# Weighted values ahead of the second softmax, norms by pairs of tiles, and four batches of head sums

## The chip, the cores and the metric

The kernel runs on one core of one Trainium2 chip. The metric is the device time of an execution in microseconds (us), as the median of several executions. Beside it there is one profiled execution, from which all durations below are taken.

The engines have the names of the profile: PE is TensorE's matmul, PEld its weight load, DVE is VectorE, ACT is ScalarE, POOL is GpSimd and SP is SyncE, which here only issues DMAs.

## The reference

The input x has 2048 rows of 640 values in bfloat16. It is normalized once, and two blocks work on the result: attention over a dilated window, and a bilinear gate. All is added to x.

```python
xn = layernorm(x)                         # 2048 x 640, no gain or offset
q, k, v = split(xn @ wqkv)                # 32 heads of 20
# each position sees 8 positions: itself and those 2, 4, ... 14 before it
logits = einsum("bhsd,bhswd->bhsw", q, kg) * 20 ** -0.5     # outside: -1e9
o = einsum("bhsw,bhswd->bhsd", softmax(logits), vg)
y = ((xn @ w_gate) * (xn @ w_up)) @ w_down                  # 640 -> 1536 -> 640
out = x + o @ wo + y
```

## The kernel before, in words

The 2048 rows are worked on as 16 tiles of 128 rows (t) for the norm and the output, and as 4 blocks of 512 rows (j) for everything between.

*Order.* No engine's order is written by hand. Every piece of work is a Task with an engine, what it reads and writes, a priority (a small number goes first) and perhaps PSUM banks; the generators (`front`, `proj_qk`, `products`, `softmax`, `weighted`, `gu`, `dn` and others) yield Tasks and conditions. When the program is built, a planner (`Sched`) keeps an estimated time for each engine, takes the Task that can start first in its estimate, by priority among those that can start about equally soon, and appends its instructions to the engine's program. Each instruction has an estimated duration (`occ`), and a DMA an estimated issue time and landing:

```python
self.t[eng] = start + (0.48 if occ is None else occ)
...
self.t_data = max(self.t_data, start + 1.2) + nbytes / 280e3
X.end = self.t_data + 0.8 + extra
```

On the chip each engine runs its program strictly in that order and waits on semaphores for what an instruction needs. Estimates decide the order and nothing else. A Task with `lock=True` is kept from overlapping, in the estimate, with another such Task on VectorE or GpSimd.

*Norm* (`front`). For each tile: two BN statistics and an aggregation on VectorE (L542, L545), a square root on ScalarE (L548), a reciprocal on VectorE (L553), from tile 6 on also minus mean times reciprocal (L556), then the normalization to XNS on VectorE (tiles 0 to 5) or ScalarE (L569). Tiles 0 to 3 are transposed by TensorE (L599), tiles 4 to 15 by transposing DMAs on SP (L632). The result is XNT.

*Projections* (L655, L687). TensorE makes QT and KT for tiles 0 to 3 singly or by pairs, for tiles 4-5 and 6-7 by pairs, and for tiles 8-11 and 12-15 by fours, and values VST by blocks. Values go through a scratch in HBM, since they are wanted shifted and with another layout (VX).

*Logits.* VectorE multiplies queries with shifted keys (L819; for j = 3 in float32 from PSUM, L864). For j = 3 GpSimd adds some of the products (L890, L908) or issues accumulating DMAs (L886). TensorE then sums over a head's values with a 32-column matrix G (L930); four such matmuls run side by side in a 128*32 form. ScalarE copies to LOG (L941).

*Softmax* (`softmax`). Two of them, for j = 0, 1 and for j = 2, 3, on VectorE and ScalarE. Then 16 small DMAs on SP move the weights into ATX, with another layout; `("atx", x)` is marked.

*Weighted values* (`weighted`, `unit`). There are 20 units u = 5 j + c. At c = 0 ScalarE copies the weights of j from ATX into two PSUM banks (L1076) that this step holds from there on. VectorE multiplies VX with them into a slot PV in float32 (L1091), GpSimd adds pairs into a slot SV in bfloat16 (L1096), and TensorE sums over four partition groups with a 32-column matrix SEL (L1144) in batches of units; ScalarE copies to OT (L1153). `BATCH = (1, 4, 9, 14, 19)` names the unit that closes a batch. SV has five slots at first; PV has two until the second softmax is done, then three.

*Gate* (`gu`). For each j, 12 pairs of chains of five matmuls (WG and WU, L1195), each chain into one PSUM bank. ScalarE copies the first into HT, HX or XNT (L660, one helper line for most copies), and VectorE multiplies the second bank onto it (L1204), or ScalarE copies the second bank to UX and GpSimd multiplies (L1221).

*Down products* (`dn`, L1277). For each output tile 12 matmuls with WD and 5 with WO into one bank, a sum with x on VectorE (L1290), and a store.

*Conditions around the change.* `calm` lets GpSimd's locked work start only while no softmax is between its logits and its end. `on_pool` sends a gate product to GpSimd after the second softmax. `vx_loads` begins when the logits of all four blocks are planned.

Of the kernel before, what the change touches and what calls it, by code (L numbers as in the profile page):

```python
# [11 lines left out]
NCH = 5  # L12
# [336 lines left out]
def build_kernel(nc, A_x, A_wqkv, A_wo, B_x, B_w_gate, B_w_up, B_w_down, out):  # L349
# [42 lines left out]
    SV += [sb(f"SV{5 + i}", [128, 4, JB], at=a_ra + i * 4096) for i in range(3)]  # L392
    sv_free = list(range(NS))
    a_sc = place[0]
# [53 lines left out]
    def mark(*k):  # L448
        done.add(k)
# [7 lines left out]
    def num(n, *k):  # L457
        return lambda: count.get(k, 0) >= n
# [4 lines left out]
    def dma(o, i, r=(), w=(), name="", eng="sp", group=None, land=None):  # L463
        n = mybir.dt.size(o.dtype)
        for s in o.shape:
# [7 lines left out]
                                         fill=1.0, base=0, channel_multiplier=1),  # L473
       r=[IDENT[:]], w=[IDENT[:]], name="ident", occ=0.4)
    op("pool", lambda e: e.memset(G[:], 0.0), w=[G[:]], name="g0", occ=0.2)
    op("pool", lambda e: e.affine_select(G[:], G[:], pattern=[[-4, H]], compare_op=ALU.is_gt,
# [57 lines left out]
    def front(t):  # L534
# [9 lines left out]
        def aggr():  # L544
            op("dve", lambda e: e.bn_aggr(mv, st), r=[("st", t, 0), ("st", t, 1)], w=[("mv", t)], name=f"bnag{t}", occ=0.2)  # L545

        def sqrt():
            op("act", lambda e: e.activation(sd, mv[:, 1:2], ACT.Sqrt, bias=EPSC[:, 0:1]), r=[("mv", t), EPSC[:]],  # L548
               w=[("sd", t)], name=f"sd{t}", occ=0.25)
            mark("sd", t)  # L550

        def recip():
            op("dve", lambda e: e.reciprocal(rstd, sd), r=[("sd", t)], w=[("rstd", t)], name=f"rstd{t}", occ=0.16)  # L553
            mark("rstd", t)
            if t >= N_DVE_A:
                op("dve", lambda e: e.tensor_scalar(nmr, mv[:, 0:1], rstd, -1.0, op0=ALU.mult, op1=ALU.mult),  # L556
                   r=[("mv", t), ("rstd", t)], w=[("nmr", t)], name=f"nmr{t}", occ=0.13)

# [25 lines left out]
        yield Task("dve", aggr, r=[("st", t, 1)], prio=p)  # L584
        yield Task("act", sqrt, r=[("mv", t)], prio=p - 1)
        yield Task("dve", recip, r=[("sd", t)], prio=p)
        if t >= NXN:
# [190 lines left out]

    def calm():
        return all(("sm", x) in done or count.get(("logits", x), 0) < 2 for x in range(2))  # L780

# [9 lines left out]
    def products():  # L791
        rows = {j: [] for j in range(NJ)}
        holds = {}
        for j, kind in ORDER:
            if kind == "w":
                if j not in holds:
                    yield from fetch(j, 0, holds.setdefault(j, {c: [] for c in range(4)}))
                yield from wide(j, rows[j], holds[j])
            else:
                if len(QUAD.get(j, ())) == 2 and j not in holds:  # L800
                    yield from fetch(j, 0, holds.setdefault(j, {c: [] for c in range(4)}))
                for r in (1, 0):
                    for c in range(NCH - 1 if r in QUAD.get(j, ()) else 0, NCH):
                        yield from narrow(j, r, c, rows[j])
            if len(rows[j]) == 10 - 3 * len(QUAD.get(j, ())):
                K.spawn(logits(j, rows[j]))

    def narrow(j, r, c, slots):
# [16 lines left out]
    def q_bank(j, c, hold):  # L825
        def go(b):
            mms([(PS[:, b, :], 0, c, j * JB, JB)], b, f"p0_{j * JB}")
            hold.append(b)
            if len(QUAD[j]) == 2:
                for _ in range(4):  # L830
                    bump("qk", 0, j, c)

        def copy():
            evac([(QT[:, j, c, :], PS[:, hold[0], :], JB)], f"qev{j}_{c}")
# [13 lines left out]
    def wide(j, slots, hold):  # L848
        halves = [(r, q0) for r in QUAD[j] for q0 in (0, 2)]
        acc, parts = {}, {1: [], 0: []}  # L850
        for c0 in (0, 2):
            for i, (r, q0) in enumerate(halves):
                f = []
                for c in (c0, c0 + 1):
                    yield lambda: len(hold[c]) > 0 and len(usable(j)) > 0
                    k = slot(j)
                    f.append(k)
                    o = PRD32[k]
                    kv, rk = k_view(j, r, c, q0, 2)
                    q = PS[:, hold[c][0], :]  # L860
                    qb = q.unsqueeze(1).to_broadcast([128, 2, JB])

                    def go(o=o, qb=qb, kv=kv, q=q, rk=rk):
                        X = op("dve", lambda e: e.tensor_tensor(o[:], qb, kv, ALU.mult), r=[q, rk], w=[o[:]],  # L864
                               name=f"prow{j}_{r}_{c}_{q0}", occ=1.17)
# [91 lines left out]
    def softmax(x):  # L957
        def tt(o, a, b, f, name, occ):
            return Task("dve", lambda: op("dve", lambda e: e.tensor_tensor(o, a, b, f), r=[a, b], w=[o], name=name, occ=occ,
                                          lock=True), r=[a, b], w=[o], prio=10, lock=True)  # L960

# [7 lines left out]
        def sub():  # L969
            op("dve", lambda e: e.tensor_tensor(L[:], L[:], bc(M3[:], 8), ALU.subtract), r=[L[:], m3], w=[L[:]], name="lsub",  # L970
               occ=1.2, lock=True)

        def exp():
            op("act", lambda e: e.activation(L[:], L[:], ACT.Exp), r=[L[:]], w=[L[:]], name="exp", occ=1.9)

        def recip():
            op("act", lambda e: e.activation(s3, s3, ACT.Ln), r=[s3], w=[s3], name="rln", occ=0.4)
            op("act", lambda e: e.activation(R, s3, ACT.Exp, scale=-1.0), r=[s3], w=[R], name="rs", occ=0.4)

        def attn():  # L980
            op("dve", lambda e: e.tensor_tensor(L[:], L[:], bc(RS[:], 8), ALU.mult), r=[L[:], R], w=[L[:], ("tok", x)], name="attn",  # L981
               occ=1.2, lock=True)

        def move():
# [6 lines left out]

        yield num(2, "logits", x)
        if x:
            yield have("sm", x - 1)
# [15 lines left out]
    NU = NJ * NCH  # L1010
    BATCH = (1, 4, 9, 14, 19)

    def vx_loads():
        yield num(NJ, "lg")
        for u in range(NU):
# [23 lines left out]
    def weighted():  # L1039
        yield have("atx", 0)  # L1040

        def take(a, b):
            at_bank.extend((a, b))

        yield Task("act", take, banks=2, prio=0, contig=True)
        for u in range(NU):
            yield from unit(u)

    def unit(u):
# [4 lines left out]
        if not more and count.get(("dn", 0), 0) >= 8:  # L1054
            more.append(1)
            sv_free.extend(range(NS, len(SV)))
        yield lambda: len(sv_free) > 0
        sv_of[u] = sv_free.pop(0)
# [13 lines left out]
        v = VX[:, u % NVX]  # L1072

        def at_copy(r):
            o, i = PS[:, at_bank[r], :], ATX[j // 2][:, j % 2, r, :]
            op("act", lambda e: e.activation(o, i, ACT.Copy), r=[i], w=[o], name=f"atp{j}_{r}", occ=0.55)  # L1076

# [31 lines left out]

        if c in (0, NCH - 1):  # L1110
            for r in range(2):
                if c == 0:
                    yield Task("act", lambda: at_copy(r), r=[ATX[j // 2][:, j % 2, r, :]],
                               w=[PS[:, at_bank[r], :]], prio=1)
# [48 lines left out]
    def on_pool(j, m):  # L1163
        return ("sm", 1) in done and m < 11 and ucount[0] - count.get(("hp",), 0) < HP_MAX

    def gu(j):
# [14 lines left out]
        for m in range(NF):  # L1181
# [17 lines left out]
            def after(h=h, hold=hold, j=j, m=m):  # L1199
# [11 lines left out]
                if on_pool(j, m):  # L1211
# [26 lines left out]
    def xr_loads():  # L1238
        yield have("xnt", NT - 1)
        yield have("vx", NVX)  # L1240
# [21 lines left out]
    def dn_piece(j, t, nb, rows, c0, c1):  # L1262
# [48 lines left out]
        K.spawn(tail())  # L1311

    N_PE_T = 4
    BN_AFTER = (4,)
    N_DVE_A = 6
    N_DVE_C = 5
# [23 lines left out]
    def misc():  # L1340
        yield have("xnt", NT - 1)

        def sel():
            for q in range(4):
                a, b = SEL[32 * q:32 * q + 32, :], IDENT[32 * q:32 * q + 32, 32 * q:32 * q + 32]
                op("dve", (lambda a, b: lambda e: e.tensor_copy(a, b))(a, b), r=[b], w=[a], name=f"sel{q}", occ=0.1)
# [5 lines left out]
        yield Task("dve", sel, prio=19)  # L1352
        yield Task("act", lambda: op("act", preload, name="exp_preload", occ=1.3), prio=6)
# [56 lines left out]
```

## Time and profile before

| what | value |
|---|---|
| median of 3 runs | 268.62 us (268.61 to 268.77) |
| the profiled execution, its own time | 268.34 us |
| its span, first to last instruction | 266.8 us |
| clock granted to TensorE | 1.000 |
| TensorE busy | 261.3 us (98%) |
| TensorE weight loads | 152.6 us (57%) |
| VectorE busy | 218.3 us (82%) |
| GpSimd busy | 132.4 us (50%) |
| ScalarE busy | 107.6 us (40%) |

The page gives busy times first, then the span in 40 slices of 6.67 us with a digit for the busy tenths of each, then the DMA queues, then the chain of work that ended last, followed back from the last instruction. In the rows of instruction groups the text before the bar names line, engine, operation, the tile written and those read, shapes and count; after the bar stand the busy time in us, the mean duration of one in ns, and the idle time of the engine just before them, with what ended it. A few per cent of matmul records are missing from a trace: a chain of five then shows four.

### The profile page before, as it was taken

Reading aid. Unit: us, or ns where it says so; the run is one execution under the profiler, and the core shown is the slowest. Engines: PE = TensorE matmul, PEld = TensorE weight load, DVE = VectorE, ACT = ScalarE, POOL = GpSimd, SP = SyncE. Lnnn points to the kernel's source line nnn. Section 1 sums busy time; section 2 is a strip of 40 time slices with the busy share of each in tenths; the row PEclk is TensorE's granted clock in tenths of the full one; section 3 lists DMA queues with packets and bytes.
Section 4 is the critical chain, followed back from the end, with each engine's and each line's share of the span. In section 5 each row is a group of like instructions: output and inputs, shape, how many; then the busy total and the mean of one; then the engine's idle time right before and its main releaser. Section 6 shows DMA issues by size and latency. Waiting matters only on the chain.

```text
span 266.8 us, 4468 instructions
## 1 busy us (share of the span) xinstructions
PE 261.3 (98%) x1771; PEld 152.6 (57%) x1788; DVE 218.3 (82%) x278; ACT 107.6 (40%) x193; POOL 132.4 (50%) x83
## 2 busy tenths in 40 slices
PE   7999999999999999999999999999999999999996
PEld 5996965444444444444444446764577547754775
DVE  4678899999999996379999899988998999981221
ACT  3469998556732122255434442007500460016000
POOL 1000000000007359700399999977999799979000
PEclk9999999999999999999999999999999999999999
DMA  7974789502226997193426733656345633130101
GB/s 213 374 207 81 195 107 371 213 0 98 101 49 161 192 234 178 9 333 81 114 49 142 170 80 87 185 162 168 80 129 152 184 96 89 49 98 2 49 27 49
DMA packets 40933, 35.75 MB, mean 134 GB/s; under 512 B 16080, under 2 KB 39120, under 8 KB 40912
## 3 DMA queue, kind: packets, MB, share of 16 engines
q1 hardware_dynamic: 40096, 33.31, 46.0%
q0 software_dynamic: 576, 2.10, 4.1%
q8 instruction: 14, 0.23, 0.4%
q10 hardware_dynamic: 240, 0.05, 0.1%
q14 instruction: 7, 0.06, 0.1%
HBM read 25.07 MB, written 5.26 MB: 114 GB/s over the span
## 4 chain that ended last, share of the span: by engine, by line
PE 96%; DVE 1%; DMA 1%; issue 1%; ACT 0%
PE PS L1195 39%; PE PS L1277 28%; PE PS L655 22%; PE PS L930 3%; PE PS L687 2%; PE PS L1144 2%; DMA XST<-in_A_x_dram 1%; PE PS L599 0%; DVE STATS L542 0%; ACT XNT L611 0%; DVE XNS L563 0%; DVE XNT L609 0%; DVE FOUT L1290 0%; ACT SD L548 0%; DVE MV L545 0%
## 5 line engine op out<-in xcount | busy, mean ns | idle before, releaser
L1096 POOL TENSOR_TENSOR SV<-PV 128x1024 bf16<-128x1024 f32 x40 | 93.2, 2361 | 20.4 <-DVE LOG L981 19.4
L1091 DVE TENSOR_TENSOR PV<-VX,PS 128x1024 f32<-128x1024 bf16 (+1 forms) x56 | 91.9, 1669 | 2.5 <-POOL SV L1096 2.3
L655 PE MATMUL PS<-XNT,WQKV 128*128 128x512 bf16 (+2 forms) x384 | 60.2, 315 | 0.4 <-issue 0.2
L1195 PE MATMUL PS<-XNT,WG 128*128 128x512 bf16 x238 | 59.4, 379 | 0.2
L1195 PE MATMUL PS<-XNT,WU 128*128 128x512 bf16 x231 | 57.7, 379 | 0.4 <-issue 0.2
L655 PEld LDWEIGHTS PS<-XNT,WQKV 128*128 128x128 bf16 x390 | 37.9, 112 | 21.8 <-ACT LOG L941 0.8
L1195 PEld LDWEIGHTS PS<-XNT,WG 128*128 128x128 bf16 x240 | 23.3, 98 | 28.5 <-issue 0.8
L1195 PEld LDWEIGHTS PS<-XNT,WU 128*128 128x128 bf16 x240 | 23.4, 98 | 28.2 <-ACT LOG L941 0.4
L819 DVE TENSOR_TENSOR PRD<-QT,KT 128x2048 bf16<-128x2048 bf16 x32 | 36.8, 1215 | 0.0
L1290 DVE TENSOR_TENSOR FOUT<-PS,XR 128x320 bf16<-128x320 f32 (+1 forms) x33 | 15.7, 477 | 18.4 <-PE PS L1277 18.3
L1277 PE MATMUL PS<-WD,HT 128*128 128x320 bf16 x192 | 28.5, 299 | 0.0
L660 ACT ACTIVATE HT<-PS 128x512 bf16<-128x512 f32 x24 | 14.3, 596 | 31.6 <-PE PS L1195 31.6
L1277 PE MATMUL PS<-WO,OT 128*128 128x320 bf16 (+1 forms) x165 | 26.6, 295 | 0.0
L890 POOL TENSOR_TENSOR PRF<-PRF,PRF 128x1024 f32<-128x1024 f32 x4 | 9.4, 2348 | 31.2 <-DVE PRF L864 31.2
L660 ACT ACTIVATE UX<-PS 128x512 bf16<-128x512 f32 x14 | 8.4, 597 | 39.5 <-PE PS L1195 39.5
L949 POOL MEMSET LOG<- 32x6 bf16 (+6 forms) x7 | 0.4, 96 | 47.6 <-ACT LOG L941 47.6
L1204 DVE TENSOR_TENSOR HT<-HT,PS 128x512 bf16<-128x512 bf16 x23 | 15.7, 684 | 9.5 <-PE PS L1195 7.4
L1277 PEld LDWEIGHTS PS<-WD,HT 128*128 128x128 bf16 x192 | 18.6, 98 | 8.0 <-issue 0.4
L1277 PEld LDWEIGHTS PS<-WO,OT 128*128 128x128 bf16 x165 | 15.9, 98 | 5.9
L864 DVE TENSOR_TENSOR PRF<-PS,KT 128x1024 f32<-128x1024 f32 x16 | 19.0, 1216 | 0.3 <-DMA PRF<-PRF 0.3
L660 ACT ACTIVATE XNT<-PS 128x512 bf16<-128x512 f32 x12 | 7.2, 598 | 25.5 <-PE PS L1195 25.5
L542 DVE BATCH_NORM_STATS2 STATS<-XST 128x6 f32<-128x320 bf16 x32 | 14.6, 472 | 2.5 <-DMA XST<-in_A_x_dram 2.5
(62 smaller groups left out, 235.7 us busy)
## 6 DMA issues: line engine op xcount, KB each, us to landing
VX<-v_scratch SPq DMA_DIRECT2D x80, 130.0 KB, 2.9
XST<-in_A_x_dram SPq DMA_DIRECT2D x16, 160.0 KB, 5.7
v_scratch<-VST SPq DMA_DIRECT2D x4, 640.0 KB, 4.2
XR<-in_A_x_dram SPq DMA_DIRECT2D x16, 160.0 KB, 2.7
out_dram<-FOUT SPq DMA_DIRECT2D x15, 160.0 KB, 1.8
PRF<-PRF POOLq DMA_DIRECT2D x4, 512.0 KB, 8.7
WG<-in_B_w_gate_dram SPq DMA_DIRECT2D x1, 1920.0 KB, 8.6
WU<-in_B_w_up_dram SPq DMA_DIRECT2D x1, 1920.0 KB, 12.0
```

Source lines behind the costliest of these rows:

```text
L542: op("dve", lambda e: e.bn_stats(o, a), r=[a], w=[("st", t, i)], name=f"bn{t}_{i}", occ=0.49)
L655: op("pe", (lambda o, l, x, c, first: lambda e: e.matmul(o, l, x, start=first, stop=(c == NCH - 1)))(o, l, x, c, first), r=[l, x], w=[o], ...
L660: X = op("act", (lambda o, i: lambda e: e.activation(o, i, ACT.Copy))(o, i), r=[i], w=[o], name=name, occ=0.12 + n * 0.9e-3)
L819: op("dve", lambda e: e.tensor_tensor(s[:], qb, kv, ALU.mult), r=[q, rk], w=[s[:]], name=f"prod{j}_{r}_{c}", occ=1.15, lock=True)
L864: X = op("dve", lambda e: e.tensor_tensor(o[:], qb, kv, ALU.mult), r=[q, rk], w=[o[:]], name=f"prow{j}_{r}_{c}_{q0}", occ=1.17)
L890: yield Task("pool", lambda: op("pool", lambda e: e.tensor_tensor(x, x, y, ALU.add), r=[x, y] + tokens(), w=[x], name=name, occ=2.36, lock ...
L1091: op("dve", lambda e: e.tensor_tensor(p, vw, a, ALU.mult), r=[vv] + rk, w=[p], name=f"pv{u}_{x}_{r0}", occ=0.09 + 1.1 * nr)
L1096: X = op("pool", lambda e: e.tensor_tensor(o, p[:, :, 0, :], p[:, :, 1, :], ALU.add), r=[p[:]] + tokens(), w=[o], name=f"pva{u}_{x}", occ= ...
L1195: op("pe", (lambda l, x, c: lambda e: e.matmul(PS[:, b, :], l, x, start=(c == 0), stop=(c == NCH - 1)))(l, x, c), r=[l, x], w=[PS[:, b, :] ...
L1204: X = op("dve", lambda e: e.tensor_tensor(h, h, PS[:, hold[1], :], ALU.mult), r=[h, PS[:, hold[1], :]], w=[h], name=f"h{m}_{j}", occ=0.65)
L1277: op("pe", (lambda l, x, i: lambda e: e.matmul(dst, l, x, start=(i == 0), stop=(i == n - 1)))(l, x, i), r=[l, x], w=[PS[:, b, :]], name=f" ...
L1290: X = op("dve", lambda e: e.tensor_tensor(o, PS[:, b, 0:wid], xr, ALU.add), r=[PS[:, b, :], xr], w=[o], name=f"fin{t}_{nb}", occ=0.15 + wi ...
```

## The change

The change has these parts:

- Head sums: `BATCH` becomes (4, 9, 14, 19), so units 0 to 4 form one batch in place of 0-1 and 2-4.
- Weighted values: `vx_loads` begins when all products have been planned; the copy of the weights for j = 0 into PSUM follows right after the two banks are taken; the slots SV3 and SV4 are handed out first and may be used before the last logits are planned.
- GpSimd beside the softmax: `calm` becomes `room(2.36)`. A GpSimd operation may be planned during the second softmax if it ends by the time (`due`) at which the next VectorE step of that softmax is expected, plus 0.3 us.
- Gate products: `on_pool` holds from the last logits on, and asks `room(1.15)`.
- Norms: for tiles 4 to 15 the square root, the reciprocal and minus mean times reciprocal are made once for two tiles.
- SEL is made on GpSimd at the start, and no longer copied from IDENT on VectorE.
- `xr_loads` waits for the last logits.
- In `products`, `q_bank` and `wide` there are additions for other settings of `ORDER` and `QUAD`; with the settings of this kernel they add no instruction.

```diff
-    sv_free = list(range(NS))
+    sv_free = [3, 4, 0, 1, 2]
...
+    op("pool", lambda e: e.memset(SEL[:], 0.0), w=[SEL[:]], name="sel", occ=0.1)
+    for q in range(4):
+        op("pool", (lambda q: lambda e: e.affine_select(SEL[:], SEL[:], pattern=[[-1, 32]], compare_op=ALU.not_equal, fill=1.0,
+                                                        base=-32 * q, channel_multiplier=1))(q),
+           r=[SEL[:]], w=[SEL[:]], name=f"sel{q}", occ=0.2)
...
+        ts = next((g for g in GROUPS if t in g), (t,))
+        t0, t1 = ts[0], ts[-1] + 1
         def sqrt():
+            o, i = SD[:, t0:t1, 0:1], MV[:, t0:t1, 1:2]
+            op("act", lambda e: e.activation(o, i, ACT.Sqrt, bias=EPSC[:, 0:1]), r=[("mv", k) for k in ts] + [EPSC[:]],
+               w=[("sd", k) for k in ts], name=f"sd{t}", occ=0.25)
...
         def recip():
+            o, i = SD[:, t0:t1, 1:2], SD[:, t0:t1, 0:1]
+            op("dve", lambda e: e.reciprocal(o, i), r=[("sd", k) for k in ts], w=[("rstd", k) for k in ts], name=f"rstd{t}", occ=0.16)
             if t >= N_DVE_A:
+                n, m = SD[:, t0:t1, 2:3], MV[:, t0:t1, 0:1]
+                op("dve", lambda e: e.scalar_tensor_tensor(n, m, -1.0, o, op0=ALU.mult, op1=ALU.mult),
...
-        yield Task("act", sqrt, r=[("mv", t)], prio=p - 1)
-        yield Task("dve", recip, r=[("sd", t)], prio=p)
+        mark("mv", t)
+        if t == ts[-1]:
+            yield Task("act", sqrt, r=[("mv", t)], prio=p - 1)
+            yield Task("dve", recip, r=[("sd", t)], prio=p)
+        yield have("rstd", t)
...
-    def calm():
-        return all(("sm", x) in done or count.get(("logits", x), 0) < 2 for x in range(2))
+    INF = 1e9
+    due = [INF]
+
+    def room(occ, ready=0.0):
+        def f():
+            if count.get(("logits", 0), 0) >= 2 and ("sm", 0) not in done:
+                return False
+            return due[0] == INF or max(K.t["pool"], K.t_lock, ready) + occ <= due[0] + SLIP
+
+        return f
+
+    calm = room(2.36)
...
-    BATCH = (1, 4, 9, 14, 19)
+    BATCH = (4, 9, 14, 19)
     def vx_loads():
-        yield num(NJ, "lg")
+        yield have("products")
...
         yield Task("act", take, banks=2, prio=0, contig=True)
+        for r in range(2):
+            yield Task("act", lambda: at_copy(0, r), r=[ATX[0][:, 0, r, :]], w=[PS[:, at_bank[r], :]], prio=1)
         for u in range(NU):
             yield from unit(u)
...
-        yield lambda: len(sv_free) > 0
+        yield lambda: len(sv_free) > 0 and (sv_free[0] in (3, 4) or count.get(("lg",), 0) >= NJ)
...
     def on_pool(j, m):
-        return ("sm", 1) in done and m < 11 and ucount[0] - count.get(("hp",), 0) < HP_MAX
+        return count.get(("lg",), 0) >= NJ and m < 11 and ucount[0] - count.get(("hp",), 0) < HP_MAX
...
-                    yield calm
+                    yield room(1.15)
...
     def xr_loads():
-        yield have("xnt", NT - 1)
+        yield num(NJ, "lg")
...
+    SLIP = 0.3
+    GROUPS = ((4, 5), (6, 7), (8, 9), (10, 11), (12, 13), (14, 15))
```

The times `due` are set in `softmax` at each of its steps: to the expected end of the step where the next one is VectorE's, and to no limit where a step of VectorE is planned whose successor is ScalarE's, or at the end.

More of the change, by code (lines that the diff above doesn't have):

```diff
@@ L545, in aggr @@
             op("dve", lambda e: e.bn_aggr(mv, st), r=[("st", t, 0), ("st", t, 1)], w=[("mv", t)], name=f"bnag{t}", occ=0.2)
+        ts = next((g for g in GROUPS if t in g), (t,))
+        t0, t1 = ts[0], ts[-1] + 1
         def sqrt():
-            op("act", lambda e: e.activation(sd, mv[:, 1:2], ACT.Sqrt, bias=EPSC[:, 0:1]), r=[("mv", t), EPSC[:]],
-               w=[("sd", t)], name=f"sd{t}", occ=0.25)
-            mark("sd", t)
+            o, i = SD[:, t0:t1, 0:1], MV[:, t0:t1, 1:2]
+            op("act", lambda e: e.activation(o, i, ACT.Sqrt, bias=EPSC[:, 0:1]), r=[("mv", k) for k in ts] + [EPSC[:]],
+               w=[("sd", k) for k in ts], name=f"sd{t}", occ=0.25)
+            for k in ts:
+                mark("sd", k)
         def recip():
-            op("dve", lambda e: e.reciprocal(rstd, sd), r=[("sd", t)], w=[("rstd", t)], name=f"rstd{t}", occ=0.16)
-            mark("rstd", t)
+            o, i = SD[:, t0:t1, 1:2], SD[:, t0:t1, 0:1]
+            op("dve", lambda e: e.reciprocal(o, i), r=[("sd", k) for k in ts], w=[("rstd", k) for k in ts], name=f"rstd{t}", occ=0.16)
             if t >= N_DVE_A:
-                op("dve", lambda e: e.tensor_scalar(nmr, mv[:, 0:1], rstd, -1.0, op0=ALU.mult, op1=ALU.mult),
-                   r=[("mv", t), ("rstd", t)], w=[("nmr", t)], name=f"nmr{t}", occ=0.13)
+                n, m = SD[:, t0:t1, 2:3], MV[:, t0:t1, 0:1]
+                op("dve", lambda e: e.scalar_tensor_tensor(n, m, -1.0, o, op0=ALU.mult, op1=ALU.mult),
+                   r=[x for k in ts for x in (("mv", k), ("rstd", k))], w=[("nmr", k) for k in ts], name=f"nmr{t}", occ=0.13)
+            for k in ts:
+                mark("rstd", k)
         def apply():
@@ L793, in products @@
         holds = {}
-        for j, kind in ORDER:
+        for at, (j, kind) in enumerate(ORDER):
             if kind == "w":
@@ L799, in products @@
             else:
-                if len(QUAD.get(j, ())) == 2 and j not in holds:
+                if len(QUAD.get(j, ())) == 2 and j not in holds and (j, "w") == ORDER[at + 1]:
                     yield from fetch(j, 0, holds.setdefault(j, {c: [] for c in range(4)}))
@@ L806, in products @@
                 K.spawn(logits(j, rows[j]))
+        mark("products")
     def narrow(j, r, c, slots):
@@ L833, in copy @@
         def copy():
-            evac([(QT[:, j, c, :], PS[:, hold[0], :], JB)], f"qev{j}_{c}")
+            o, i = QT[:, j, c, :], PS[:, hold[0], :]
+            op("act", lambda e: e.activation(o, i, ACT.Copy), r=[i], w=[o, ("qev", j, c)], name=f"qev{j}_{c}", occ=0.58)
             for _ in range(4):
@@ L855, in wide @@
                     yield lambda: len(hold[c]) > 0 and len(usable(j)) > 0
+                    yield num(4, "qk", 0, j, c)
                     k = slot(j)
@@ L863, in go @@
                     def go(o=o, qb=qb, kv=kv, q=q, rk=rk):
-                        X = op("dve", lambda e: e.tensor_tensor(o[:], qb, kv, ALU.mult), r=[q, rk], w=[o[:]],
+                        X = op("dve", lambda e: e.tensor_tensor(o[:], qb, kv, ALU.mult), r=[q, rk, ("qev", j, c)], w=[o[:]],
                                name=f"prow{j}_{r}_{c}_{q0}", occ=1.17)
@@ L958, in tt, with go @@
         def tt(o, a, b, f, name, occ):
-            return Task("dve", lambda: op("dve", lambda e: e.tensor_tensor(o, a, b, f), r=[a, b], w=[o], name=name, occ=occ,
-                                          lock=True), r=[a, b], w=[o], prio=10, lock=True)
+            def go():
+                X = op("dve", lambda e: e.tensor_tensor(o, a, b, f), r=[a, b], w=[o], name=name, occ=occ, lock=True)
+                due[0] = INF if name == "ssum3" else X.end
+            return Task("dve", go, r=[a, b], w=[o], prio=10, lock=True)
         L = LOG[x]
@@ L971, in sub @@
                occ=1.2, lock=True)
+            due[0] = INF
         def exp():
-            op("act", lambda e: e.activation(L[:], L[:], ACT.Exp), r=[L[:]], w=[L[:]], name="exp", occ=1.9)
+            X = op("act", lambda e: e.activation(L[:], L[:], ACT.Exp), r=[L[:]], w=[L[:]], name="exp", occ=1.9)
+            due[0] = X.end
         def recip():
             op("act", lambda e: e.activation(s3, s3, ACT.Ln), r=[s3], w=[s3], name="rln", occ=0.4)
-            op("act", lambda e: e.activation(R, s3, ACT.Exp, scale=-1.0), r=[s3], w=[R], name="rs", occ=0.4)
+            X = op("act", lambda e: e.activation(R, s3, ACT.Exp, scale=-1.0), r=[s3], w=[R], name="rs", occ=0.4)
+            due[0] = X.end
         def attn():
@@ L982, in attn @@
                occ=1.2, lock=True)
+            due[0] = INF
         def move():
@@ L992, in softmax @@
         yield num(2, "logits", x)
+        if x:
+            due[0] = max([0.0] + [d.end for d in K.deps_of("dve", K.keys(L[:]), ()).values()])
         if x:
@@ L1045, in weighted, with at_copy @@
         yield Task("act", take, banks=2, prio=0, contig=True)
+        for r in range(2):
+            yield Task("act", lambda: at_copy(0, r), r=[ATX[0][:, 0, r, :]], w=[PS[:, at_bank[r], :]], prio=1)
         for u in range(NU):
             yield from unit(u)
+    def at_copy(j, r):
+        o, i = PS[:, at_bank[r], :], ATX[j // 2][:, j % 2, r, :]
+        op("act", lambda e: e.activation(o, i, ACT.Copy), r=[i], w=[o], name=f"atp{j}_{r}", occ=0.55)
     def unit(u):
@@ L1072, in unit @@
         v = VX[:, u % NVX]
-        def at_copy(r):
-            o, i = PS[:, at_bank[r], :], ATX[j // 2][:, j % 2, r, :]
-            op("act", lambda e: e.activation(o, i, ACT.Copy), r=[i], w=[o], name=f"atp{j}_{r}", occ=0.55)
         def mul(x, r0, nr):
@@ L1108, in adder @@
             yield Task("pool", lambda: add(x), r=[slots[x][:]], w=[sv[:, 2 * x:2 * x + 2, :]], prio=10, lock=True)
-        if c in (0, NCH - 1):
+        if c == NCH - 1 or (c == 0 and j):
             for r in range(2):
                 if c == 0:
-                    yield Task("act", lambda: at_copy(r), r=[ATX[j // 2][:, j % 2, r, :]],
+                    yield Task("act", lambda: at_copy(j, r), r=[ATX[j // 2][:, j % 2, r, :]],
                                w=[PS[:, at_bank[r], :]], prio=1)
@@ L1341, in misc @@
         yield have("xnt", NT - 1)
[L1343 to L1346, printed above, removed]
         def preload(e):
@@ L1351, in misc @@
         free.append(NPR - 1)
-        yield Task("dve", sel, prio=19)
         yield Task("act", lambda: op("act", preload, name="exp_preload", occ=1.3), prio=6)
```

## The prediction

> **What bounds the kernel now.** I read the page's table of busy time first, then its slices, then the chain of waits, then TensorE's timeline around the places where the change acts. The page first: busy shares, the slices of three engines, and the chain by engine and by line.
>
> ```profile
> PE 261.3 (98%) x1771; PEld 152.6 (57%) x1788; DVE 218.3 (82%) x278; ACT 107.6 (40%) x193; POOL 132.4 (50%) x83
> PE   7999999999999999999999999999999999999996
> DVE  4678899999999996379999899988998999981221
> POOL 1000000000007359700399999977999799979000
> PE 96%; DVE 1%; DMA 1%; issue 1%; ACT 0%
> PE PS L1195 39%; PE PS L1277 28%; PE PS L655 22%; PE PS L930 3%; PE PS L687 2%; PE PS L1144 2%; DMA XST<-in_A_x_dram 1%; PE PS L599 0%; DVE STATS L542 0%; ACT XNT L611 0%; DVE XNS L563 0%; DVE XNT L609 0%; DVE FOUT L1290 0%; ACT SD L548 0%; DVE MV L545 0%
> ```
>
> TensorE has work in every slice, and 96% of the chain that ends last is TensorE's own. VectorE and GpSimd have holes in slices 15 to 19 (100 to 131 us), which is where the change puts work. But no TensorE time lies behind those holes. Busy TensorE is not yet TensorE at its peak, so I checked the pace in its timeline (columns: start, us, engine, line, operation, tiles, count).
>
> ```profile
> 140.47 1.03 PE L1195 MATMUL PS<-XNT,WU 128*128 128x512 bf16 x4
> 141.64 0.61 PE L1144 MATMUL PS<-SV,SEL 128*32 128x512 bf16 x8
> 142.19 1.25 PE L1195 MATMUL PS<-XNT,WG 128*128 128x512 bf16 x5
> ...
> 157.31 1.24 PE L1195 MATMUL PS<-XNT,WG 128*128 128x512 bf16 x5
> 158.39 1.24 PE L1195 MATMUL PS<-XNT,WU 128*128 128x512 bf16 x5
> 159.56 0.83 PE L1144 MATMUL PS<-SV,SEL 128*32 128x512 bf16 x12
> 160.32 1.80 PE L1277 MATMUL PS<-WD,HT 128*128 128x320 bf16 x12
> ...
> 187.44 1.24 PE L1195 MATMUL PS<-XNT,WG 128*128 128x512 bf16 x5
> 188.61 1.26 PE L1144 MATMUL PS<-SV,SEL 128*32 128x512 bf16 x20
> 189.81 3.43 PE L1277 MATMUL PS<-WD,HT 128*128 128x320 bf16 x24
> ```
>
> A chain of five gate matmuls starts every 1.08 us (157.31 to 158.39), and does so all the way; a piece of x4 is a chain with one record missing. From the first projections at 8.46 us on, the starts follow each other without a hole, so the order on TensorE hides everything else. What it loses is at each visit to the narrow form (128*32): L930 four times for the logits, L1144 five times for the head sums. The end, from the chain in order of time:
>
> ```profile
> 244.42 1.19 PE PS L1144 x20
> 245.61 18.64 PE PS L1277 x153
> 264.25 0.02 issue
> 264.27 0.33 DVE FOUT L1290
> ```
>
> After the last matmul come one sum on VectorE and a store, up to 266.8. So the span is the start-up (about 8.5 us), TensorE's stream (about 255.8) and an end (2.5).
>
> **What the Trainium skill says.** "Perfetto Trace Analysis", section Identifying the Most-Contended Engine, says that matmul occupancy is no measure of the distance from the peak; the chain pitch above is the check, and here it is steady. "TensorEngine Tiling (Array Packing)", section Key Properties, says that a change of tiling mode drains the array; the trace agrees, with about 0.2 us a visit (next part). "SBUF — State Buffer", section Who interferes with whom, says that a VectorE instruction with two SBUF inputs excludes a GpSimd instruction that reads SBUF, while TensorE and ScalarE wait for nobody; the kernel's lock keeps the two apart, so no row of this trace shows the price.
>
> **The change part by part.**
>
> *Four batches of head sums.* The 80 matmuls stay; one visit goes. A visit lasts from the end of the chain before (its start plus 1.08) to the next start: 8 matmuls 142.19 - 141.55 = 0.64 us; 12 take 160.32 - 159.47 = 0.85; 20 take 189.81 - 188.52 = 1.29. That is 0.055 us a matmul and 0.19 to 0.20 a visit. Two visits (0.64 + 0.85 = 1.49) become one of 1.29: **-0.20 us**, on the path. Then the down products of tile j = 0 follow this batch directly, as they follow the ones at 188.61 and 217.02, whose batches have five units too and cost no hole. It needs five free banks at once, as those do.
>
> *Weighted values ahead of the second softmax, and the waiting rule for GpSimd (room).* Nothing is removed. The muls of units 0 and 1 (four of 1.213 us and two of 2.278) can start on VectorE when the products on KT end, at about 103 us, instead of 115.44, because their operands have landed by then; VectorE is busy only 5.43 and 6.18 us in the windows 100 to 110 and 110 to 120. GpSimd, idle from 111.7 to 131.05 (19.4 us waiting for LOG of L981), can take three or four adds of 2.361 us there: it gets ahead by 7 to 9 us. **0 on the path**: TensorE's chains cover it, since no start of theirs waits for an add or a mul. If that cover were gone, an add is worth up to 2.36. On GpSimd an add may stand before a PRF sum (2.35) of the last logits, so L930 of j = 3 (114.66) may come up to 2.4 us later; gate chains stand ready: that too costs 0.
>
> *The copy of attention weights into PSUM (PS<-ATX, L1076), tile 0.* Two instructions of 0.597 us move from 114.18 and 116.30 to the moment the planner expects ATX. This adds a wait at the head of ScalarE's queue. Behind it stand the evacuations HT, one each 2.16 us. The 16 moves go out over SP from 72.21 to 82.61, and the last lands 1.9 us after its issue at 82.0, at 83.9. The planner counts 0.48 us an issue; the trace shows 10.40 / 16 = 0.65, so ScalarE may arrive (16 x 0.17 =) 2.7 us early. It has slack: the evacuation at 83.47 would become about 85.1, while its bank is wanted again at about 86.5 (four chains in four free banks, 8 less two for weights and two for queries). I take 0, bounds 0 to 1.5 us.
>
> *Earlier loads of VX.* Their issue on SP (16 of them from 83.37) already follows the last reader of QT, and WD and WO stay behind on SP; 0. XR's new condition: 0, its first use is after 160.
>
> *Norms of two tiles.* For tiles 4 to 15, six square roots (0.287), six reciprocals (0.163) and five of ten nmr (0.214) go: ScalarE gains 1.7 us of busy time, VectorE 2.0, in 15 to 37 us, where ScalarE is at 19.47 of 20. The first tile of a pair is 1 to 1.5 us later, the second about where it was; TensorE always waits for the second (its groups are of tiles 4-5, 6-7, 8-11, 12-15), so 0 is my value. The nearest margins: tile 5's XNT lands at 21.3 and its first chain starts at 24.19; tile 11's transpose, issued at 30.62, lands up to 4.3 us later (34.9), and the chain starts at 35.32, a margin of 0.4. The two transposes of a pair now go out back to back, 1.28 us each on SP. Bounds: -0 (no start there waits now) to +0.8.
>
> *SEL on GpSimd.* Four VectorE copies of 0.164 at 36.9 go; a memset and four selects of about 0.21, with 0.28 between starts, are added at 1.5 us. G and the pad of KT come 1.2 us later, wanted much later; the first statistics at 3.15 would run beside the last of them. No row shows whether that slows either: 0, bounds 0 to 0.2.
>
> *Gate products on GpSimd sooner.* A product of 0.684 on VectorE becomes an evacuation of 0.597 and one of 1.156 on GpSimd, in time idle on both: 0.
>
> Sum: -0.20, against the profiled execution's 268.34 us (span 266.8 and 1.54 around it): 268.14. That execution is 0.28 below the median of the three runs, 268.62, so the median would be **268.4 us**. What a measurement of this kernel can tell from no change is about 0.2%, 0.54 us, so my forecast is a change too small to tell.
>
> **Rivals.**
>
> *A: a wait takes the place of the visit, slower.* The new head-of-queue wait on ScalarE for ATX. For it: the planner's 0.48 against 0.65 measured, and 83.9 as the landing. Against: the bank margin of about 2.4 us (84.07 to 86.5). It decides from the point where the copy ends over 2.4 us after the evacuation would have; with ATX or its plan another 1.5 us worse, TensorE stops 1.5 us: 269.9.
>
> *B: XNT of a second tile late.* The margin of 0.4 at 35.32 is used up by back-to-back transposes; 0.3 to 0.8 us: about 268.9.
>
> *C: the batch doesn't save its visit,* because the planner finds no five free banks there and TensorE idles as long as it gains: 268.6.
>
> *D: faster.* VectorE and GpSimd were the hidden bound at the end: the sums at 244.36 follow the last gate chain at once and the last add ended at 244.4. If earlier sums let the order close up by half an add more: 268.4 - 1.2 = 267.2. Against: no hole on TensorE there to close.
>
> **How the numbers follow.** Main case 58% (268.1 to 268.8), C 10%, B 12% (a third of it beyond 269.16), A 16% (to 271), D 4%. Faster by over 0.2%: D, 0.04. Slower: A and a third of B, 0.20. Within: the rest, 0.76. The range from 268.1 to 269.5 takes in the main case, B, C and the milder part of A, and leaves out D and the rest of A, some 16%.
>
> **What would show it.** Four L1144 visits of 20, no idle TensorE from 8.5 us to its last matmul, which ends about 264.05; a GpSimd add before 130 us; PS<-ATX at about 84; six fewer SD on ScalarE. The steps are wrong if TensorE waits on a bank near 84 to 88, or on XNT near 24 or 35. The whole is wrong if the span differs by over 0.6 us either way with TensorE's stream unbroken.

## The result: 1.2% slower, and the profile after

| | before | after |
|---|---|---|
| median of 4 runs | 268.69 us (268.61 to 269.02) | 272.02 us (271.67 to 272.43) |
| profiled execution, its span | 268.34, 266.8 us | 271.67, 270.1 us |

The ratio is 1.0122, with a 95% interval from 1.0105 to 1.0140: slower by 3.3 us, where 268.4 us had been forecast. The page of the changed kernel, in the rows that answer to those shown of before:

```profile
PE 261.8 (97%) x1771; PEld 152.5 (56%) x1788; DVE 214.4 (79%) x254; ACT 109.3 (40%) x194; POOL 142.0 (53%) x95
PE   7999999999998999999899999999999999999996
DVE  4687899999986989599996979979998999711221
POOL 3000000000062289993379998799986999775000
PE 72%; DVE 9%; ACT 6%; POOL 5%; SPq 3%; issue 2%; DMA 2%; DVEq 0%
```

Three things changed. TensorE has two slices with an 8 (81 to 88 us and 128 to 135 us). Its share of the last chain fell from 96% to 72%: the chain now leaves TensorE for other engines. GpSimd now works between 108 and 122 us, where it had rested from 111.7 us on, as the change intends. The busy share alone, 98% to 97%, would hardly have shown the loss: a matmul's end is modelled, and about 0.16 us of a stop counts as busy (the first stop below, of 1.23 us, has an idle time of 1.07).

The intended gain is there. From the chain in order of time:

```profile
182.30 1.19 PE PS L1184 x20
...
211.79 1.19 PE PS L1184 x20
...
240.19 1.19 PE PS L1184 x20
...
267.60 0.33 DVE FOUT L1330
```

Head sums (now L1184) stand in batches of 20. The first batch, at 148.5 us, is not whole on this chain; it is one visit in place of two. What costs time is three stops of TensorE. I measure a stop as the start of a piece in TensorE's timeline, less the start of the piece before it and that piece's pace (1.08 us a chain, 1.29 a visit of 20).

**Stop 1, 1.23 us.** TensorE's and ScalarE's timelines (start, us, engine, line; in brackets the idle time before, and what ended it):

```profile
81.25 1.24 PE L1235 MATMUL PS<-XNT,WU 128*128 128x512 bf16 x5
83.56 2.35 PE L671 MATMUL PS<-XNT,WQKV 128*128 128x512 bf16 x10 [1.07 <-ACT HT L676]
```
```profile
78.22 0.60 ACT L676 ACTIVATE VST<-PS 128x512 bf16<-128x512 f32 x1 [0.57 <-PE PS L671]
81.88 1.12 ACT L1091 ACTIVATE PS<-ATX 128x512 f32<-128x512 bf16 x2 [3.06 <-DMA ATX<-LOG]
82.93 1.06 ACT L676 ACTIVATE HT<-PS 128x512 bf16<-128x512 f32 x2
```

ScalarE stands 3.06 us at the copies PS<-ATX (L1091), until the last DMA has landed. Two evacuations HT, whose chains are done, stand behind the copies. So TensorE has no free bank, and its start at 83.56 should have been at 82.33 (81.25 + 1.08).

**Stop 2, 1.12 us in three parts** (0.65 at 131.7, 0.33 at 133.1, 0.14 at 136.5). VectorE's, GpSimd's and ScalarE's timelines, in the second softmax. First the two steps on VectorE in the kernel before:

```profile
119.40 0.75 DVE L959 TENSOR_TENSOR M<-M 128x512 bf16<-128x512 bf16 x2
...
124.03 1.23 DVE L959 TENSOR_TENSOR SM<-LOG 128x1024 f32<-128x1024 bf16 x1 [0.25 <-ACT LOG L974]
```

Then the changed kernel:

```profile
117.20 0.69 DVE L989 TENSOR_TENSOR M<-LOG 128x1024 bf16<-128x1024 bf16 x1
117.92 3.61 DVE L989 TENSOR_TENSOR M<-M 128x512 bf16<-128x512 bf16 x2
...
126.11 3.00 DVE L989 TENSOR_TENSOR SM<-LOG 128x1024 f32<-128x1024 bf16 x1
```
```profile
117.37 2.73 POOL L1136 TENSOR_TENSOR SV<-PV 128x1024 bf16<-128x1024 f32 x1 [0.43 <-DVE PV L1131]
120.06 1.33 POOL L1261 TENSOR_TENSOR HT<-HT,UX 128x512 bf16<-128x512 bf16 x1
125.67 2.35 POOL L1136 TENSOR_TENSOR SV<-PV 128x1024 bf16<-128x1024 f32 x1 [4.29 <-DVE PV L1131]
```
```profile
130.32 0.42 ACT L1011 ACTIVATE SM<-SM 128x256 f32<-128x256 f32 x1 [3.63 <-DVE SM L989]
...
131.09 1.55 ACT L676 ACTIVATE HT<-PS 128x512 bf16<-128x512 f32 x3
```

Two small maxima that took 0.75 us before take 3.61, and a sum that took 1.23 takes 3.00. Each time GpSimd works beside them. The first maximum (2.45 of the 3.61 us) runs beside the add of 117.37, the second (1.12) beside the gate product of 120.06, and the sum beside the add of 125.67. These steps are then late; ScalarE waits 3.63 us for the last sum at L1011, and three evacuations HT stand behind it. They end the first part of the stop. The other two parts end with gate products on VectorE, which come late behind the same sums.

**Stop 3, 0.99 us**, in the first batch of head sums:

```profile
148.51 1.26 PE L1184 MATMUL PS<-SV,SEL 128*32 128x512 bf16 x18
150.38 0.39 PE L1184 MATMUL PS<-SV,SEL 128*32 128x512 bf16 x2 [0.61 <-POOL SV L1136]
150.70 3.43 PE L1317 MATMUL PS<-WD,HT 128*128 128x320 bf16 x24
```
```profile
137.69 4.67 POOL L1136 TENSOR_TENSOR SV<-PV 128x1024 bf16<-128x1024 f32 x2 [1.66 <-DVE LOG L1016]
...
145.65 4.67 POOL L1136 TENSOR_TENSOR SV<-PV 128x1024 bf16<-128x1024 f32 x2
```

The chain before ends at 148.42 (147.34 + 1.08). The batch takes 150.70 - 148.42 = 2.28 us instead of 1.29, since the last add of unit 4 ends only at 150.3. GpSimd in turn had waited for the late softmax, until 137.69. In sum: 1.23 + 1.12 + 0.99 - 0.20 for the visit, and 0.14 from x, which landed 0.2 us later in this execution, make 3.28 of the 3.3 us of span.

### The profile page after: what moved, and what is told of

It reads as the page before. It is cut to its first block, busy times and chain, and to the rows that moved or that the text cites. A ratio compares the mean times of both kernels' runs of the same rounds, so it can differ in the third digit from the quotient of the medians.

```text
span 270.1 us, 4455 instructions
## 1 busy us (share of the span) xinstructions
PE 261.8 (97%) x1771; PEld 152.5 (56%) x1788; DVE 214.4 (79%) x254; ACT 109.3 (40%) x194; POOL 142.0 (53%) x95
## 4 chain that ended last, share of the span: by engine, by line
PE 72%; DVE 9%; ACT 6%; POOL 5%; SPq 3%; issue 2%; DMA 2%; DVEq 0%
PE PS L1235 30%; PE PS L1317 27%; PE PS L671 9%; DVE PRD L846 4%; POOL SV L1136 3%; SPq L467 3%; ACT XNS L582 3%; PE PS L703 2%; PE PS L1184 1%; PE PS L959 1%; DMA XST<-in_A_x_dram 1%; DVE SM L989 1%; DVE LOG L1016 1%; POOL HT L1261 1%; DVE PV L1131 1%
## 5 line engine op out<-in xcount | busy, mean ns | idle before, releaser
L676 ACT ACTIVATE UX<-PS 128x512 bf16<-128x512 f32 x21 | 12.6, 600 | 25.4 <-PE PS L1235 23.5
L676 ACT ACTIVATE HX<-PS 128x512 bf16<-128x512 f32 x12 | 7.2, 597 | 26.7 <-PE PS L1235 26.6
L1244 DVE TENSOR_TENSOR HT<-HT,PS 128x512 bf16<-128x512 bf16 x20 | 13.4, 681 | 4.6 <-ACT HT L676 3.3
```

The lines of the kernel that those rows point to most:

```text
L676: X = op("act", (lambda o, i: lambda e: e.activation(o, i, ACT.Copy))(o, i), r=[i], w=[o], name=name, occ=0.12 + n * 0.9e-3)
L1244: X = op("dve", lambda e: e.tensor_tensor(h, h, PS[:, hold[1], :], ALU.mult), r=[h, PS[:, hold[1], :]], w=[h], name=f"h{m}_{j}", occ=0.65)
```

## Experiments

All ratios are to runs of the kernel before on the same chip.

**The copies later in ScalarE's queue.** After planning, two instructions are moved in ScalarE's program; nothing else moves. They come to stand behind the third HT evacuation (three later, not two).

`later` is a helper that takes the named operations out of the planned list and puts them behind another one; its lines are left out here.

```diff
+    later(("atp0_0", "atp0_1"), "gev2_0")
     K.emit(stores)
```

> The changed kernel with one difference: in ScalarE's program the two copies PS<-ATX of j = 0 stand two HT evacuations later; every other engine's program is as before. Theory 1 (one cause): the wait of 3.06 us for ATX at the head of ScalarE's queue stops TensorE for 1.23 us near 82 us, and also makes VectorE and GpSimd late (first GpSimd add at 109.8, softmax at 117.2), so that GpSimd adds run into the softmax steps near 118 and 126 us and TensorE stops again near 131 and 149. Then all three stops go or nearly go: about 268.6 to 269.2 us. Theory 2 (separate causes): only the first stop goes: 272.0 - 1.2 = 270.8 us, with about 2.0 us of stops left near 131 and 149.

Measured: 270.44 us (ratio 1.0065, 1.0049 to 1.0082). Stop 1 is gone, and the others stay, with the same 3.61 and 3.00 us steps. Theory 2 holds: the causes are separate. The evacuation that had stood behind the copies now runs at 79.32 us.

**No GpSimd work in the second softmax.**

```diff
-    calm = room(2.36)
+    def calm():
+        return all(("sm", x) in done or count.get(("logits", x), 0) < 2 for x in range(2))
...
-                    yield room(1.15)
+                    yield calm
```

> The changed kernel with the old condition on GpSimd's work (none between the logits and the end of the second softmax). Theory 1 (GpSimd's adds exclude VectorE's softmax steps: 3.61 us for two steps that took 0.75, and 3.00 for one that took 1.23): those steps are back at 0.75 and 1.23, the stop near 131 (1.1 us) goes; the stop of 1.23 near 82 stays; the one at the first head sums (0.95) may shrink or stay: 270 to 270.9 us. Theory 2 (the stop near 131 comes from ScalarE's or VectorE's order of work, not from GpSimd): no change there, 272 us or more.

Measured: 269.93 us (1.0051, 1.0036 to 1.0066). The steps are back at 0.75 and 1.22 us. Stops 2 and 3 are both gone, and only stop 1 is left, with 1.40 us. So stop 3 goes with GpSimd's work in the softmax: here a batch of five units waits for nothing.

**Five batches again**, in the changed kernel.

```diff
-    BATCH = (4, 9, 14, 19)
+    BATCH = (1, 4, 9, 14, 19)
```

> The changed kernel with five batches of head sums, as before the change. Theory 1 (the stop of 0.95 us in the first batch of five units is the price of asking for all five at once): it goes, one visit comes back at 0.20: about 271.2 us. Theory 2 (the stop has its cause in GpSimd's lateness, and any batch that ends with unit 4 waits for it): it stays near 150 us and the time becomes 272.2.

Measured: 274.31 us (1.0213, 1.0198 to 1.0229), further up than either theory said. The first small batch now stands in the softmax and brings new stops (0.92 and 0.74 us near 124); stop 1 is 1.51 us here, and stop 2 is 0.79. The stop at unit 4's sums stays, as theory 2 has it, and grows:

```profile
149.76 1.24 PE L1235 MATMUL PS<-XNT,WU 128*128 128x512 bf16 x5
150.93 0.82 PE L1184 MATMUL PS<-SV,SEL 128*32 128x512 bf16 x10
152.83 0.39 PE L1184 MATMUL PS<-SV,SEL 128*32 128x512 bf16 x2 [1.07 <-POOL SV L1136]
153.50 1.80 PE L1317 MATMUL PS<-WD,HT 128*128 128x320 bf16 x12 [0.28 <-DVE HX L1244]
```

This batch of three units takes 153.50 - 150.84 = 2.66 us, where 0.85 is its pace. So stop 3 does not need a batch of five. The run does not isolate the price of the visit.

**Norms by pairs alone**, in the kernel before (the edits of `front` and `GROUPS`).

> The kernel before with the norms of tiles 4 to 15 by pairs and nothing else of the change. Theory: TensorE always waits for the second tile of a pair or for none, so no stop arises: 268.6 +- 0.2 us. Rival: XNT of tile 5 or 11 comes late and TensorE stops near 24 or 35 us: 268.9 to 269.5 us.

Measured: 268.50 us (1.0001, 0.9992 to 1.0009), no stop near 24 or 35 us. The pairs cost and bring nothing that these runs can tell.

**Both suspects undone** (the first two edits together).

> The changed kernel with both suspects undone: the two copies PS<-ATX two HT evacuations later, and no GpSimd work between the logits and the end of the second softmax. The four batches, the norms by pairs and SEL stay. Theory 1 (these two are all): no stop of TensorE after 8.6 us, the saved visit shows: 268.2 to 268.4 us beside 268.5 for the kernel before. Theory 2 (a third stop at the first batch comes back once TensorE reaches it earlier): 268.6 to 269.4 us, with the stop near 148.

Measured: 268.43 us (0.9992, 0.9984 to 1.0000); no stop. From the second tile's projections to the end of the last matmul TensorE takes 255.56 us (before 255.77): the visit of 0.21 us.

**Adds or gate products.** Copies later; the adds may run in the softmax, and the products were meant to wait for its end.

```diff
-                    yield room(1.15)
+                    yield calm
```

> Copies later; GpSimd's adds of weighted values may run in the second softmax as changed, its gate products wait for the end of it. Theory 1 (an add of 2.36 us that reads SBUF holds up a softmax step on VectorE, and the rest follows): the stops near 130 and 148 stay, 270.2 to 270.6 us, as with both kinds of work (270.44). Theory 2 (the gate products, with their evacuations UX on ScalarE, make the stop): 268.3 to 268.8 us.

Measured: 270.45 us (1.0067, 1.0053 to 1.0081), as with both kinds of work. But this run does not decide between the theories, because its edit does not do what was expected of it. In the changed kernel `calm` is `room(2.36)`, no longer the old condition, so a product may still be planned in the softmax. GpSimd's timeline shows one there:

```profile
116.26 2.73 POOL L1136 TENSOR_TENSOR SV<-PV 128x1024 bf16<-128x1024 f32 x1 [0.44 <-DVE PV L1131]
118.95 1.33 POOL L1261 TENSOR_TENSOR HT<-HT,UX 128x512 bf16<-128x512 bf16 x1
```

VectorE, ScalarE, GpSimd and SP work in the same order as with the copies later alone, so this is that kernel measured again. How the delay is shared can be read from the changed kernel's trace: beside the two adds the steps lose 2.02 us (2.45 - 0.43) and 1.77 us (3.00 - 1.23), beside the product 0.83 us (1.12 - 0.29). Theory 2 is answered by the run with the planned order made real, below: the products and their evacuations UX stand in the softmax there too, and nothing stops. What a kernel with the adds alone would take was not measured.

**Do reads exclude each other?** In the kernel before, GpSimd gets work in the softmax, from 116.6 us on; the other engines' programs stay as they were. First four sums of UX in SBUF:

```diff
+                op("pool", lambda e: e.memset(UX[:], 0.0), w=[UX[:]], name="probe0", occ=0.0)
+                for i in range(4):
+                    op("pool", lambda e: e.tensor_tensor(UX[:], UX[:], UX[:], ALU.add), r=[UX[:]] + [d], w=[UX[:]], ...)
```

> The kernel before with five GpSimd instructions added, nothing else moved in any program: after the last logits a memset of UX (128x1536 bf16) and four sums UX + UX, which read SBUF, while GpSimd would be idle (111.7 to 131 us). Theory 1 (a GpSimd instruction that reads SBUF excludes VectorE instructions with two SBUF inputs): the softmax steps of 0.69, 0.75 (two), 1.22 and 1.23 us on VectorE stretch by some of the 3 to 4 us that a sum lasts, by 3 us or more in all. Theory 2 (no exclusion; the long steps had another cause): they keep their durations within 0.1 us.

and then memsets in the place of the four sums:

> The same with twenty one memsets of UX, which only write SBUF, in place of the sums. Theory 1 (reads alone exclude): the softmax steps keep 0.69, 0.75, 1.22 and 1.23 us. Theory 2 (any GpSimd instruction excludes): they stretch as with the sums.

The sums start after the last logits because they name LOG (d) as read. So the step that writes LOG waits for all of them, and the times of these two kernels (274.22 and 291.57 us) are not used, only the steps ahead of that wait. VectorE, then GpSimd, with the sums:

```profile
118.68 1.17 DVE L963 TENSOR_TENSOR M<-LOG 128x1024 bf16<-128x1024 bf16 x1
119.88 5.61 DVE L963 TENSOR_TENSOR M<-M 128x512 bf16<-128x512 bf16 x2
125.41 0.68 DVE L1208 TENSOR_TENSOR HT<-HT,PS 128x512 bf16<-128x512 bf16 x1
```
```profile
116.55 11.61 POOL L947 TENSOR_TENSOR UX<-UX 128x1536 bf16<-128x1536 bf16 x4 [3.56 <-ACT LOG L941]
```

and the same with the memsets:

```profile
118.79 0.69 DVE L963 TENSOR_TENSOR M<-LOG 128x1024 bf16<-128x1024 bf16 x1
119.51 0.75 DVE L963 TENSOR_TENSOR M<-M 128x512 bf16<-128x512 bf16 x2
```
```profile
116.64 28.65 POOL L947 MEMSET UX<- 128x1536 bf16 x20 [3.54 <-ACT LOG L941]
```

The maxima take 1.17 and 5.61 us beside sums, 0.69 and 0.75 beside memsets. A gate product beside the sums, which reads one operand from PSUM, keeps its 0.68. Theory 1 holds in both, as far as the steps go that run ahead of that wait.

**The planner told the issue time**, without GpSimd work in the softmax and without a move by hand.

```diff
-                    dma(d, src, r=[src], w=[d], name=f"atx{x}_{a}{q}", group=f"atx{x}_{a // 2}")
+                    dma(d, src, r=[src], w=[d], name=f"atx{x}_{a}{q}", group=f"atx{x}_{a // 2}", occ=0.65)
```

> The changed kernel without GpSimd work in the second softmax, and with one estimate changed: the planner counts 0.65 us, the measured pitch, for the issue of each of the sixteen DMAs into ATX, instead of 0.48. Nothing is moved by hand; the planner itself now puts the copies PS<-ATX behind the first HT evacuation and ahead of the second. Theory 1 (the wrong issue time alone put the copies where they stop TensorE): the stop of 1.40 us near 82 goes, 268.3 to 268.6 us. Theory 2 (landing is later than planned for another reason too): the copies still wait, and a stop of 0.3 to 1.4 us stays, 268.7 to 269.9.

Measured: 268.34 us (0.9990, 0.9982 to 0.9999), no stop. ScalarE and TensorE:

```profile
79.35 0.60 ACT L676 ACTIVATE HT<-PS 128x512 bf16<-128x512 f32 x1 [0.48 <-PE PS L1236]
82.21 1.12 ACT L1092 ACTIVATE PS<-ATX 128x512 f32<-128x512 bf16 x2 [2.26 <-DMA ATX<-LOG]
83.27 0.58 ACT L676 ACTIVATE HT<-PS 128x512 bf16<-128x512 f32 x1
```
```profile
81.31 1.24 PE L1236 MATMUL PS<-XNT,WU 128*128 128x512 bf16 x5
82.39 2.32 PE L671 MATMUL PS<-XNT,WQKV 128*128 128x512 bf16 x10
```

The copies still wait 2.26 us (theory 2 was right in that), but one evacuation now stands ahead of them, and TensorE goes on at 82.39 without a hole. The wait is not the cost; what stands behind it is.

**The planned order made real.** Copies later, GpSimd's work in the softmax as changed; each softmax step on VectorE and each add or gate product on GpSimd waits for the one of the other engine that is planned ahead of it (the same two marks also at the subtraction, the last product and the gate product).

```diff
-                X = op("dve", lambda e: e.tensor_tensor(o, a, b, f), r=[a, b], w=[o], name=name, occ=occ, lock=True)
+                X = op("dve", lambda e: e.tensor_tensor(o, a, b, f), r=[a, b, ("gp", x)], w=[o, ("step", x)], name=name, occ=occ, lock=True)
...
-            X = op("pool", lambda e: e.tensor_tensor(o, p[:, :, 0, :], p[:, :, 1, :], ALU.add), r=[p[:]] + tokens(), w=[o],
+            X = op("pool", lambda e: e.tensor_tensor(o, p[:, :, 0, :], p[:, :, 1, :], ALU.add), r=[p[:], ("step", 1)] + tokens(), w=[o, ("gp", 1)],
```

> The changed kernel with the copies two HT evacuations later, GpSimd's adds and products in the second softmax as changed, and the planned order between them and VectorE's softmax steps made real: each waits for the one planned ahead of it. Theory 1 (the loss comes from drift: GpSimd starts an add earlier in relation to VectorE than planned, and blocks a step): no step stretches (0.75 and 1.22 us again), the stops near 130 and 148 shrink to less than half, 268.4 to 269.4 us. Theory 2 (the room itself is too small: with 2.36 us adds between the steps the softmax is late however they are ordered): the stretch turns into idle time ahead of the steps, the stops stay, 270 to 270.8 us.

Measured: 268.32 us (0.9988, 0.9981 to 0.9995), no stop after the start. VectorE and GpSimd:

```profile
116.94 0.75 DVE L989 TENSOR_TENSOR M<-M 128x512 bf16<-128x512 bf16 x2
...
122.66 1.23 DVE L989 TENSOR_TENSOR SM<-LOG 128x1024 f32<-128x1024 bf16 x1 [0.31 <-POOL HT L1261]
```
```profile
119.03 2.36 POOL L1136 TENSOR_TENSOR SV<-PV 128x1024 bf16<-128x1024 f32 x1 [2.97 <-DVE LOG L1002]
```

The add that ran from 117.37 in the changed kernel now waits 2.97 us for the step L1002, as planned, and runs beside ScalarE's exponential. The second softmax's weights are ready at 132.4 us instead of 137.6. VectorE, ScalarE, GpSimd and SP work in the same order as with the copies later alone (270.44 us); only the waits between VectorE and GpSimd are new. Theory 1 holds: the room was there, but nothing on the chip kept the planned order between the two engines.

**The whole change with both repairs** (issue time and real order).

> The changed kernel whole (four batches, pairs, SEL, copies and GpSimd work in the second softmax), with two repairs: the planner counts 0.65 us for the issue of a DMA into ATX, and the planned order of GpSimd's work and VectorE's softmax steps is made real. Theory 1 (these are the two causes): no stop after 8.6 us, one visit saved: 0.2 us under the kernel before, 268.2 to 268.5 us. Theory 2 (the two repairs disturb each other): a stop of over 0.3 us somewhere, 268.7 or more.

Measured: 268.35 us (0.9992, 0.9985 to 0.9998), no stop. This keeps every part of the change and is 0.2 us under the kernel before, as was forecast for the change itself.

## Why the prediction was wrong

**The visit** (-0.20 us) was right: 0.21 in each of the four kernels without stops that have four batches. The **pairs** at nothing were right by their own run. **SEL** and the **earlier loads** have no run of their own; the whole change with both repairs keeps them, has no stop and gains the visit, so nothing of them is seen there. One reading was off: ScalarE's 19.47 of 20 us belongs to the window from 20 to 40 us, and nothing came of it.

**The copy was the first step that failed, by the evacuation it chose: 1.23 us where 0 was taken.** The wait was estimated at 2.7 us and was 3.06; the margin of a bank, 2.4 us, was right too. But the text took the evacuation at 83.47 us as the one behind the copies, late by 1.6. In the changed order the last DMA lands at 81.9, not 83.9, and the evacuation due at 79.3 stood behind the copies. It ran at 82.93, 3.6 us late, and 3.6 - 2.4 = 1.2 is the stop of 1.23. Even in the trace of before an evacuation stood at 81.31, the very time at which ScalarE was reckoned to arrive at the copies (83.9 - 2.7 = 81.2):

```profile
81.31 0.60 ACT L660 ACTIVATE HT<-PS 128x512 bf16<-128x512 f32 x1 [1.65 <-PE PS L1195]
83.47 0.60 ACT L660 ACTIVATE HT<-PS 128x512 bf16<-128x512 f32 x1 [1.56 <-PE PS L1195]
```

It was passed over. Rival A named this wait, with a stop of 1.5 us, at 16%.

**"0 on the path" for GpSimd's work beside the softmax was the second, and the larger: 2.1 us.** Two sentences carried it. One said that the kernel's lock keeps VectorE and GpSimd apart. The lock holds in the planner's estimates only; nothing on the chip waits for it, and while VectorE's first maximum came at 117.20, the add had nothing to wait for but its own input. The exclusion that "SBUF — State Buffer", section Who interferes with whom, describes was quoted without a price; here it was 2.9 us on two steps (3.61 - 0.75) and 1.8 on a third. Of this, 0.83 us came beside a gate product, which had been taken at 0 as well. The other sentence said that no TensorE start waits for an add or a mul. That was read from the order of before. The path went round: a late softmax step holds ScalarE's Ln, the Ln holds three HT evacuations, and these hold the banks. And the first batch of sums waits for an add directly (0.99 us).

**Rival C** had the first batch waiting, for lack of banks; it waited 0.99 us, for adds. **Rivals B and D** did not happen. None of the cases summed two stops, and the range ended at 269.5.

## What to carry to other kernels

When one engine is full and every other hides behind it, look at the in-order queue of the engine that frees its buffers: for an instruction moved into that queue, list what stands directly behind it in the new order, and compare its lateness with the buffer margin. A planner's lock that is not a semaphore protects only as long as nothing drifts; two engines that exclude each other need a real wait, or time to spare. Correct the estimates that a plan rests on (0.48 us planned for the issue of a DMA, 0.65 measured before and 0.70 after the change) before more is packed into the plan.

## What was not expected of the hardware

Two VectorE maxima of 0.43 and 0.29 us, both inputs in SBUF, took 2.45 and 1.12 us beside a GpSimd add and a gate product, and 2.85 and 2.72 us beside the larger sums of UX. In these traces whichever of the two instructions started first kept its time, and the other ended late. The two maxima end 0.3 and 0.15 us after the add and the product beside them, and the softmax sum of 1.23 us ends 1.1 us after its add (129.11 against 128.02). Each time that is the step's own length less about 0.14 us. So a GpSimd instruction that reads SBUF can hold a short VectorE step for several of its lengths.

It goes the other way as well. The add of 117.37 started while the first maximum still ran, until 117.89, and took 2.73 us instead of 2.36. In the kernel with five batches again, a gate product that started at 128.98, while a softmax sum ran until 130.11, took 2.14 us instead of 1.16. Memsets on GpSimd and VectorE operations with one PSUM operand stayed at their durations.
